# Loading attention pairs over 128 partitions instead of 96, and requesting two FFN weights later

## The chip, the cores and the metric

The kernel runs on one NeuronCore of a Trainium2 chip. The metric is the device time of one execution in microseconds (us). TensorE (PE in the profile) does matrix products and transposes, and loads its stationary operand with separate instructions (PEld). VectorE (DVE), ScalarE (ACT) and GpSimd (POOL) do elementwise work. SyncE (SP) and GpSimd issue most DMA transfers. SBUF is the on-chip memory with 128 partitions, and PSUM holds what TensorE writes.

## The reference

Attention with "beacon" keys and values ahead of the ordinary ones, and then a feed-forward network (FFN) that takes the maximum of three projections:

```python
B, H, S, Nb, D = 8, 8, 576, 16, 64
k_all, v_all = concat(beacon_k, k), concat(beacon_v, v)       # 592 keys
scores = q @ k_all.T / sqrt(D)                                # causal mask on the 576 ordinary keys
a = exp(scores - max); a /= a.sum() + 1e-9
x = heads_joined(a @ v_all)                                   # 4608 tokens x 512
h = maximum(maximum(x @ w1, x @ w2), x @ w3)                  # 4608 x 768
out = h @ w_out                                               # 4608 x 512
```

All inputs and the output are float32. The kernel computes in bfloat16 with float32 sums.

## The kernel before

The unit of attention is a pair: two heads of one batch, 32 pairs in all, four to a batch (`PPB`). Two pairs make a quad. For a pair, q and k must lie with the head dimension along the partitions: two heads of 64 fill 128 partitions, so `qT` is 128 x 576 and `kT` is 128 x 592 (beacons first). There are four of each (`NT`), used in turn.

The pairs get there in three ways. Batch 0 (pairs 0 to 3) is loaded in halves and turned on TensorE by `turn_half`. Pairs 4 to 15 (batches 1 to 3; `B_PE` is 4) are loaded by `load_pair` (L172), cast to bfloat16 by GpSimd in `cast_piece` (L215), turned on TensorE in `turn` (L344), and copied out of PSUM by `evac_q` and `evac_k` (L382, L392). Pairs 16 to 31 use the same load and cast, are stored to DRAM in bfloat16 and fetched by a transposing DMA (L328 to L340).

For a pair of the second kind, partition p of 96 (`QP`) holds six consecutive tokens (`QR`) of both heads. Each token slot r is turned as a 96 x 128 block, so q and k take six transposes each; the copy out of PSUM puts the tokens back in order by a strided view.

The scores of a pair are made in four groups (`emit_scores`, L442): matmuls into one of two PSUM buffers named `sc`, then an exponential on ScalarE. GpSimd zeroes the masked part with affine_select (`emit_masks`, L467, L480). `emit_pv` (L500) multiplies the exponentials with ones, for the sums, and with the values (L524); `invert_sums` and `multiply` divide, and write the FFN's input `xT`. FFN units follow as their tokens become ready: `mm1_halves` (L603) for the first two weights of token block 0, `mm1_unit` (L584) for the rest, and `mm2_unit` (L620) for the output product. For block 0, the first L584 unit is the first that reads the third weight, and the first L620 the first that reads `w_out_sb`.

The order on every engine is written out by hand. `first_steps` (L794) is the list for batch 0. After it, each pair p from 4 has two steps, (p, 0) and (p, 1); in each come the scores of two groups, their masks, a part of `emit_pv` of an earlier quad, then transposes, FFN units and what `plan` holds for that step. In step (p, 0), `turn_pair` turns pair p + 1. Each engine carries out its own instructions in this order and waits at semaphores for the others. GpSimd runs masks, casts and the issues of the weight DMAs on one queue: `load_w` (L282) issues two DMAs for one of the three weights, `load_w_out` (L289) one. All pair loads, value loads and output stores are issued by SyncE, in the order of the list `loads` (L702): pairs 4 and 5, then pair 6, the values of batch 1, and pairs 7 and on. A stage buffer `st` (eight of them) holds one pair or part of the values of a batch.

Of the kernel before, what the change touches and what calls it, by code (L numbers as in the profile page):

```python
# [9 lines left out]
BF16 = mybir.dt.bfloat16  # L10
# [6 lines left out]
def kernel(  # L17
# [13 lines left out]
    nc = tc.nc  # L31

    B, H, S, D = q.shape
    Nb = beacon_k.shape[2]
    NK = S + Nb
    scale = 1.0 / float(D) ** 0.5
    d_model, d_ff = moe_w1.shape
# [6 lines left out]

    QR = 6
    QP = S // QR
    HR = QR // 2
    HALF = S // 2  # L50


    n_kt = (NK + 127) // 128
    NKP = 128 * n_kt
# [5 lines left out]
    PPB = H // 2  # L60
# [4 lines left out]
    B_PE = 4  # L65
# [55 lines left out]
    ffn_psum = ctx.enter_context(tc.tile_pool(name="ffn_psum", bufs=2, space=PSUM))  # L121
# [16 lines left out]
    ident = const.tile([128, 128], BF16, name="ident")  # L138
# [2 lines left out]


    NT = 4
    qTs = [const.tile([128, S], BF16, name=f"qT{i}") for i in range(NT)]
    kTs = []
    for i in range(NT):
        z = const.tile([128, NKP], BF16, name=f"kT{i}")
        nc.vector.memset(z[:, NK:NKP], 0.0)
        nc.vector.memset(z[:, Nb + HALF : 384], 0.0)
        kTs.append(z)  # L150
    nc.vector.memset(ones, 1.0)
    tri = const.tile([128, 128], BF16, name="tri")

    def pv_bank(i, shape, dtype):
        return pv_psum.tile(shape, dtype, name=f"pv{i}")
# [3 lines left out]
    by_pool = nc.gpsimd.tensor_copy  # L159

    STW = 4 * QR * D
    NQ2 = 2 * QR * D
    stage = {}
    v_tiles = {}

    def new_stage(key):
        stage[key] = st_pool.tile([128, STW], FP32, name="st")
        return stage[key]  # L170

    def load_pair(p, gate=None):  # L172
        b, g, j0 = place(p)
        hs = slice(head(g, j0), head(g, j0) + 2)
        st = new_stage(("pair", p))

        if gate:
            gate.memset(st[0:QP, 0:1], 0.0)
        for i, src in enumerate((q, k)):
            nc.sync.dma_start(  # L180
                out=st[0:QP, i * NQ2 : (i + 1) * NQ2].rearrange("p (h x) -> p h x", h=2),
                in_=src[b, hs].rearrange("h (p r) d -> p h (r d)", r=QR),
            )
# [28 lines left out]
            for j in range(PPQ):  # L212
                stage["half16", PPQ * g + j, h, i] = t16[:, 2 * j : 2 * j + 2]

    def cast_piece(p, i, cast):  # L215
        st = stage["pair", p]
        t16 = pair_pool.tile([QP, QR, 2, D], BF16, name=f"p16{i}")
        cast(  # L218
            t16.rearrange("p r h d -> p h r d"),
            st[0:QP, i * NQ2 : (i + 1) * NQ2].rearrange("p (h r d) -> p h r d", h=2, r=QR),  # L220
        )
        stage["pair16", p, i] = t16

    def cast_pair(p, q_cast, k_cast):
        cast_piece(p, 0, q_cast)
        cast_piece(p, 1, k_cast)
        stage.pop(("pair", p))

    V_PIECES = [(0, 3), (3, n_kt)]

# [111 lines left out]


    def turn(p, i, ps):  # L344
        src = stage.pop(("pair16", p, i))
        for r in range(QR):
            nc.tensor.transpose(  # L347
                ps[:, r * QP : (r + 1) * QP],
                src[:, r].rearrange("p h d -> p (h d)"),
                ident[0:QP, 0:QP],  # L350
            )

    def fill(ps, n):
        for i in range(n):
            x0 = 512 + 128 * (i % 4)
            nc.tensor.transpose(ps[:, x0 : x0 + 128], busy[:, 0:128], ident)
# [24 lines left out]

    def evac_q(p, ps, copy):  # L382
        copy(
            qTs[p % NT].rearrange("d (p r) -> d p r", r=QR),
            ps.rearrange("d (r p) -> d p r", r=QR),
        )

    def place_beacons(p, copy):
        b, pi = divmod(p, PPB)
        copy(kTs[p % NT][:, 0:Nb], bT[:, pi, Nb * b : Nb * (b + 1)])  # L390

    def evac_k(p, ps, copy):  # L392
        kT = kTs[p % NT]
        copy(
            kT[:, Nb:NK].rearrange("d (p r) -> d p r", r=QR),
            ps.rearrange("d (r p) -> d p r", r=QR),
        )

    def turn_apart(p, i):
        ps = ffn_psum.tile([128, S], BF16, name="fps")  # L400
        turn(p, i, ps)
        (evac_q, evac_k)[i](p, ps, by_dve)
        if i == 1:
            place_beacons(p, by_act)

    def turn_pair(p, q_copy, shared=True):
        if shared:
            ps = sc_psum.tile([128, 2, 1024], BF16, name="sc")
            banks = [ps[:, i, 0:S] for i in range(2)]
        else:  # L410
            banks = [pv_bank(i, [128, 1024], BF16)[:, 0:S] for i in range(2)]
        for i in range(2):
            turn(p, i, banks[i])
        evac_k(p, banks[1], by_dve)
        evac_q(p, banks[0], q_copy)
# [283 lines left out]
    def load_pairs(p0, p1):  # L699
        return [L(load_pair, p) for p in range(p0, p1)]  # L700
# [79 lines left out]
    def G(p):  # L780
        return L(load_pair, p, nc.vector)
# [7 lines left out]
    def F(n):  # L789
        return lambda: [emit_ffn(END) for _ in range(n)]  # L790
# [16 lines left out]
        ((2, 3), [P(0, 1, False, 0, 2), F(1), M(2, 3)]),  # L807
        ((3, 1), [P(0, 1, False, 2, 4), M(3, 1, True), G(5), F(1), L(turn_beacons, 1, B_PE, bk16_1)]),
        ((3, 2), [F(1), finish_pv, next_7, M(3, 2)]),
        ((3, 3), [F(2), M(3, 3), L(cast_pair, 4, by_pool, by_pool), L(load_w, 2, 0, d_ff), P(1, 1),  # L810
                  L(turn_apart, 4, 0), L(turn_apart, 4, 1), finish_pv, F(1), L(cast_pair, 5, by_pool, by_pool)]),
    ]
    at_step(4, 0, C(cast_pair, 6, by_pool, by_pool))
    at_step(5, 0, C(cast_v, 1, 0, by_pool))
    at_step(5, 0, L(load_w_out))
    at_step(5, 1, C(cast_v, 1, 1, by_pool))
    at_step(5, 1, C(cast_pair, 7, by_pool, by_pool))
    for p in range(8, B_PE * PPB):
        at_step(p - 2, 1, C(cast_pair, p, by_pool, by_pool))
    for b in range(2, B):  # L820
        p = b * PPB
# [6 lines left out]
    for b in range(B_PE, B):  # L828
        p = b * PPB
# [9 lines left out]
    def emit_all():  # L839
# [107 lines left out]
```

## Time and profile before

| What | Value |
|---|---|
| Time, median of 5 runs | 302.04 us (301.32 to 307.57) |
| Profiled execution: time, span | 301.66 us, 299.9 us |
| Mean granted TensorE clock | 0.989 |
| TensorE busy | 284.6 us (95%) |
| GpSimd busy | 127.6 us (43%) |
| L347 transposes of pairs 4 to 15 | 12 a pair |
| L218 casts of a pair's half on GpSimd | 822 ns each, 56 of them |
| L394 copy of k from PSUM (VectorE) | 754 ns |
| L383 copy of q from PSUM (ScalarE) | 640 ns |
| Third weight (two DMAs): issued, median to landing | 31.29 and 31.84 us, 8.8 us |
| Output weight: issued, to landing | 43.90 us, 14.1 us |

Times inside the execution count from the start of the span. "Idle before" is the time for which an engine stood before an instruction, with what released it. The granted clock is the share of TensorE's full clock that the chip allowed. A group's mean is the length of one instruction; matmuls overlap, so their start-to-start distance is shorter than that.

### The profile page before, as it was taken

What the parts mean: (1) busy time and instruction counts of PE and PEld (TensorE: products, weight loads), DVE (VectorE), ACT (ScalarE), POOL (GpSimd) and SP (SyncE); (2) the same over time, 40 slices, a digit from 0 to 9 for tenths busy, and PEclk for the clock granted to TensorE, in tenths of its full rate; (3) what the DMA queues carried; (4) which work ended last, traced back from release to release, by engine and by line L of the source; (5) the groups of instructions that cost most, each with busy time, mean ns of one, the idle gap of its engine ahead of it and who ended that gap; (6) DMA issues with size and microseconds to landing.
All of it is one profiled execution on the core that took longest, in us unless ns stands there. A gap on an engine that the chain in (4) does not pass through costs nothing.

```text
span 299.9 us, 8667 instructions
## 1 busy us (share of the span) xinstructions
PE 284.6 (95%) x3571; PEld 154.6 (52%) x3601; DVE 172.4 (57%) x343; ACT 146.6 (49%) x237; POOL 127.6 (43%) x253
## 2 busy tenths in 40 slices
PE   8879969999999999999999999999999999999995
PEld 4547645554554545454545777545454544444442
DVE  3756633545767475636573757465746575274373
ACT  3685673875665564536463646354635531401300
POOL 7182855566566584556455545552243210000000
PEclk9999995999999999999999999999999999999999
DMA  8999999999999999999999999993212001103003
GB/s 145 186 183 229 213 222 249 256 225 289 217 252 240 210 286 181 192 194 304 235 186 218 298 242 185 153 264 88 42 52 90 2 3 68 74 1 123 19 0 141
DMA packets 85321, 50.68 MB, mean 169 GB/s; under 512 B 64417, under 2 KB 80033, under 8 KB 85281
## 3 DMA queue, kind: packets, MB, share of 16 engines
q1 hardware_dynamic: 80672, 45.76, 69.4%
q0 software_dynamic: 4048, 4.03, 8.2%
q8 instruction: 28, 0.46, 0.7%
q10 hardware_dynamic: 560, 0.33, 0.5%
q14 instruction: 13, 0.10, 0.1%
HBM read 35.13 MB, written 14.22 MB: 165 GB/s over the span
## 4 chain that ended last, share of the span: by engine, by line
PE 82%; DMA 9%; ACT 2%; DVE 2%; POOL 2%; issue 1%; SPq 0%; POOLq 0%; DVEq 0%
PE fps L584 31%; PE sc L584 12%; PE pv L524 12%; PE fps L620 11%; PE sc L452 8%; DMA st<-in_v_dram 4%; PE sc L620 4%; DMA quad<-in_k_dram 3%; DMA st<-in_k_dram 2%; ACT at_sb L461 2%; PE sc L347 2%; DVE xT L556 1%; POOL quad L209 1%; DVE y L628 1%; PE fps L603 1%
## 5 line engine op out<-in xcount | busy, mean ns | idle before, releaser
L461 ACT ACTIVATE at_sb<-sc 128x928 bf16<-128x928 f32 (+5 forms) x128 | 103.9, 863 | 83.7 <-PE sc L452 83.1
L584 PE MATMUL fps<-xT,w_sb 128*128 128x512 bf16 (+1 forms) x464 | 107.1, 358 | 2.2 <-issue 1.0
L480 POOL TENSOR_SCALAR_AFFINE_SELECT at_sb<-at_sb 128x256 bf16<-128x256 bf16 (+2 forms) x148 | 53.8, 382 | 99.5 <-ACT at_sb L461 99.5
L584 PEld LDWEIGHTS <-w_sb 128*128 128x128 bf16 x672 | 61.8, 98 | 65.8 <-issue 12.9
L594 DVE TENSOR_TENSOR hT<-hT,fps 128x512 bf16<-128x512 bf16 x70 | 48.0, 687 | 29.8 <-PE fps L584 29.5
L218 POOL CAST p<-st 96x768 bf16<-96x768 f32 x56 | 44.6, 822 | 0.9 <-DMA st<-in_q_dram 0.5
L584 PE MATMUL sc<-xT,w_sb 128*128 128x512 bf16 (+1 forms) x187 | 42.9, 356 | 0.1
L452 PE MATMUL sc<-qT,kT 64*128 64x288 bf16 (+5 forms) x400 | 35.8, 277 | 2.3 <-ACT at_sb L461 2.2
L620 PE MATMUL fps<-w_out_sb,hT 128*128 128x512 bf16 x143 | 34.6, 379 | 0.9 <-issue 0.6
L620 PEld LDWEIGHTS <-hT 128*128 128x128 bf16 x210 | 19.9, 98 | 24.0 <-DVE hT L594 2.1
L594 DVE TENSOR_TENSOR hT<-hT,sc 128x512 bf16<-128x512 bf16 x32 | 22.0, 688 | 16.9 <-PE sc L584 11.3
L628 DVE COPY y<-fps 128x512 f32<-128x512 f32 x25 | 17.3, 692 | 23.5 <-PE fps L620 22.9
L592 DVE CAST hT<-fps 128x512 bf16<-128x512 f32 x32 | 22.1, 691 | 12.3 <-PE fps L584 12.2
L524 PE MATMUL pv<-at_sb,v_sb 128*32 128x288 bf16 (+5 forms) x1376 | 29.1, 231 | 0.0
L556 DVE TENSOR_TENSOR xT<-pv,recip 128x288 bf16<-128x288 f32 (+2 forms) x93 | 27.2, 347 | 2.7 <-ACT recip L546 2.7
L452 PEld LDWEIGHTS <-kT 64*128 64x128 bf16 x400 | 14.4, 94 | 26.7 <-issue 23.0
L524 PEld LDWEIGHTS <-v_sb 128*32 128x32 bf16 (+1 forms) x1408 | 24.7, 97 | 2.0 <-issue 0.6
L524 PE MATMUL pv<-at_sb,ones 128*32 128x288 bf16 (+4 forms) x500 | 17.6, 256 | 2.5 <-POOL at_sb L480 2.5
L263 POOL CAST v_sb<-st 128x1536 bf16<-128x1536 f32 (+2 forms) x21 | 18.4, 893 | 3.1 <-DMA st<-in_v_dram 3.1
L544 ACT ACTIVATE lnd<-pv 128x288 f32<-128x288 f32 x31 | 13.0, 418 | 10.7 <-PE pv L524 10.7
L524 PEld LDWEIGHTS <-ones 128*32 128x32 bf16 (+2 forms) x512 | 10.9, 95 | 10.0 <-issue 8.3
L592 ACT CAST hT<-sc 128x512 bf16<-128x512 f32 x6 | 3.5, 587 | 23.7 <-PE sc L584 23.7
(74 smaller groups left out, 163.9 us busy)
## 6 DMA issues: line engine op xcount, KB each, us to landing
out_dram<-y SPq DMA_DIRECT2D x35, 256.0 KB, 3.5
st<-in_q_dram SPq DMA_DIRECT2D x28, 288.0 KB, 5.9
st<-in_k_dram SPq DMA_DIRECT2D x28, 288.0 KB, 6.3
st<-in_v_dram SPq DMA_DIRECT2D x24, 256.0 KB, 5.4
w_sb<-in_moe_w_dram POOLq DMA_DIRECT2D x6, 384.0 KB, 7.0
q_dram<-p SPq DMA_DIRECT2D x16, 144.0 KB, 3.2
k_dram<-p SPq DMA_DIRECT2D x16, 144.0 KB, 2.7
st<-in_v_dram SPq DMA_DIRECT2D x8, 224.0 KB, 5.5
```

The costliest lines, as they stand in the source:

```text
L218: cast(t16.rearrange("p r h d -> p h r d"), st[0:QP, i * NQ2 : (i + 1) * NQ2].rearrange("p (h r d) -> p h r d", h=2, r=QR),)
L263: cast(v_sb[0:n, t:t1].rearrange("p t h d -> p (t h d)"), st[0:n, (t - t_lo) * H * D : (t1 - t_lo) * H * D],)
L452: nc.tensor.matmul(ps[:, e, off : off + q1 - q0], kT[hs, 128 * t : 128 * t + 128], qT[hs, q0:q1], start=True, stop=True, tile_position=(64 ...
L461: nc.scalar.activation(out=both_heads(p, gi), in_=ps[:, :, 0 : g_width(p, gi)], func=AF.Exp, scale=scale)
L480: nc.gpsimd.affine_select(out=view, in_=view, compare_op=ALU.is_ge, fill=0.0, base=x0, pattern=[[0, 2], [1, hi - lo]], channel_multiplier=-1,)
L524: nc.tensor.matmul(ps[bank][32 * j : 32 * j + 32, lo + q0 - qa : lo + qb - qa], lhsT, at_view(PPQ * quad + j // 2, t, j % 2, q0, qb), star ...
L556: nc.vector.tensor_mul(xT[:, 2 * g + part - 1, c0 + ca : c0 + cb], ps[bank][:, lo : lo + cb - ca], recip[:, ca:cb],)
L584: nc.tensor.matmul(ps[:, o0 : o0 + n], w_in[i][:, ct, 128 * ft : 128 * (ft + 1)], xT[:, ct, x0 : x0 + n], start=(ct == 0), stop=(ct == n_c ...
L592: (by_act if alone[0] else by_dve)(h, ps)
L594: nc.vector.tensor_max(h, h, ps)
L620: nc.tensor.matmul(ps, hT[:, ft, 128 * tt : 128 * (tt + 1)], w_out_sb[:, ft, :], start=(ft == 0), stop=(ft == n_ft - 1),)
L628: nc.vector.tensor_copy(y, ps)
```

## The change

It has two parts.

The first is the layout of pairs 4 to 15. A load now puts tokens 0 to 511 on all 128 partitions, four consecutive tokens to a partition (`WR` = 4, 1 KB of a head in one run instead of 1.5 KB), for q and for k. The last 64 tokens (`REST`) of q go to partitions 0 to 63, and those of k to partitions 64 to 127 of the same columns. A pair takes four DMAs instead of two. GpSimd casts it with three instructions: q, k, and the common rest. TensorE turns four full 128 x 128 blocks of q, and then four of k and the common one. The copies out of PSUM are one for q's 512 columns, one for k's 512, and one with two pieces of 64 columns for both rests; for that, `qT` and `kT` are now views of one tile `qkT`. Pairs 16 to 31 keep their layout, in a cast tile that now holds q and k together.

The second is the order on GpSimd's queue. The third weight is requested at step (4, 1), after that step's masks, instead of between the casts of pairs 4 and 5. The output weight is requested at step (6, 0) instead of (5, 0).

```diff
+    WR = 4
+    WIDE = 128 * WR
+    REST = S - WIDE
...
-    qTs = [const.tile([128, S], BF16, name=f"qT{i}") for i in range(NT)]
...
+    qkTs = [const.tile([128, S + NKP], BF16, name=f"qkT{i}") for i in range(NT)]
+    qTs = [z[:, 0:S] for z in qkTs]
+    kTs = [z[:, S : S + NKP] for z in qkTs]
...
+    def load_wide(p, gate=None):
...
+        W = 2 * WR * D
+        for i, src in enumerate((q, k)):
+            nc.sync.dma_start(
+                out=st[:, i * W : (i + 1) * W].rearrange("p (h x) -> p h x", h=2),
+                in_=src[b, hs, 0:WIDE].rearrange("h (p r) d -> p h (r d)", r=WR),
+            )
+        for i, src in enumerate((q, k)):
+            nc.sync.dma_start(
+                out=st[REST * i : REST * (i + 1), 2 * W : 2 * W + 2 * D].rearrange("p (h d) -> p h d", h=2),
+                in_=src[b, hs, WIDE:S].rearrange("h p d -> p h d"),
+            )
+
     def load_pair(p, gate=None):
+        if p < B_PE * PPB:
+            load_wide(p, gate)
+            return
...
+    def cast_wide(p, cast):
+        st = stage.pop(("pair", p))
+        t16 = pair_pool.tile([128, 2 * QR, 2, D], BF16, name="p16")
+        W = 2 * WR * D
+        for i in range(2):
+            cast(
+                t16[:, WR * i : WR * (i + 1)].rearrange("p r h d -> p h r d"),
+                st[:, i * W : (i + 1) * W].rearrange("p (h r d) -> p h r d", h=2, r=WR),
+            )
+        cast(t16[:, 2 * WR].rearrange("p h d -> p (h d)"), st[:, 2 * W : 2 * W + 2 * D])
+        stage["wide16", p] = t16
...
     def turn(p, i, ps):
-        src = stage.pop(("pair16", p, i))
-        for r in range(QR):
+
+        src = stage["wide16", p]
+        slots = [(r, WR * i + r) for r in range(WR)] + ([(WR, 2 * WR)] if i == 1 else [])
+        for r, slot in slots:
             nc.tensor.transpose(
-                ps[:, r * QP : (r + 1) * QP],
-                src[:, r].rearrange("p h d -> p (h d)"),
-                ident[0:QP, 0:QP],
-            )
+                ps[:, r * 128 : (r + 1) * 128],
+                src[:, slot].rearrange("p h d -> p (h d)"),
+                ident,
+            )
...
     def evac_k(p, ps, copy):
-        kT = kTs[p % NT]
         copy(
-            kT[:, Nb:NK].rearrange("d (p r) -> d p r", r=QR),
-            ps.rearrange("d (r p) -> d p r", r=QR),
+            kTs[p % NT][:, Nb : Nb + WIDE].rearrange("d (p r) -> d p r", r=WR),
+            ps[:, 0:WIDE].rearrange("d (r p) -> d p r", r=WR),
         )
+        step = S + Nb
+        x0 = S + NKP - 2 * step
+        copy(
+            qkTs[p % NT][:, x0:].rearrange("d (i x) -> d i x", i=2)[:, :, WIDE - x0 : S - x0],
+            ps[:, WIDE : WIDE + 2 * REST].rearrange("d (i x) -> d i x", i=2),
+        )
...
-        ((3, 3), [F(2), M(3, 3), L(cast_pair, 4, by_pool, by_pool), L(load_w, 2, 0, d_ff), P(1, 1),
+        ((3, 3), [F(2), M(3, 3), L(cast_pair, 4, by_pool, by_pool), P(1, 1),
...
-    at_step(5, 0, L(load_w_out))
+    at_step(4, 1, L(load_w, 2, 0, d_ff))
...
+    at_step(6, 0, L(load_w_out))
```

More of the change, by code (lines that the diff above doesn't have):

```diff
@@ L143 @@
     NT = 4
-    qTs = [const.tile([128, S], BF16, name=f"qT{i}") for i in range(NT)]
-    kTs = []
-    for i in range(NT):
-        z = const.tile([128, NKP], BF16, name=f"kT{i}")
+    qkTs = [const.tile([128, S + NKP], BF16, name=f"qkT{i}") for i in range(NT)]
+    qTs = [z[:, 0:S] for z in qkTs]
+    kTs = [z[:, S : S + NKP] for z in qkTs]
+    for z in kTs:
         nc.vector.memset(z[:, NK:NKP], 0.0)
         nc.vector.memset(z[:, Nb + HALF : 384], 0.0)
-        kTs.append(z)
     nc.vector.memset(ones, 1.0)
@@ L170, in new_stage @@
         return stage[key]
+    def load_wide(p, gate=None):
+        b, g, j0 = place(p)
+        hs = slice(head(g, j0), head(g, j0) + 2)
+        st = new_stage(("pair", p))
+        if gate:
+            gate.memset(st[:, 0:1], 0.0)
+        W = 2 * WR * D
[9 more added lines that the diff above has]
+            )
     def load_pair(p, gate=None):
+        if p < B_PE * PPB:
+            load_wide(p, gate)
+            return
         b, g, j0 = place(p)
@@ L213, in load_quad @@
                 stage["half16", PPQ * g + j, h, i] = t16[:, 2 * j : 2 * j + 2]
[L215 to L220, printed above, removed]
-        )
-        stage["pair16", p, i] = t16
-    def cast_pair(p, q_cast, k_cast):
-        cast_piece(p, 0, q_cast)
-        cast_piece(p, 1, k_cast)
-        stage.pop(("pair", p))
+    def cast_wide(p, cast):
[9 more added lines that the diff above has]
+        stage["wide16", p] = t16
+    def cast_pair(p, q_cast, k_cast):
+        if p < B_PE * PPB:
+            cast_wide(p, q_cast)
+            return
+        st = stage.pop(("pair", p))
+        t16 = pair_pool.tile([128, 2 * QR, 2, D], BF16, name="p16")
+        for i, cast in enumerate((q_cast, k_cast)):
+            part = t16[0:QP, QR * i : QR * (i + 1)]
+            cast(
+                part.rearrange("p r h d -> p h r d"),
+                st[0:QP, i * NQ2 : (i + 1) * NQ2].rearrange("p (h r d) -> p h r d", h=2, r=QR),
+            )
+            stage["pair16", p, i] = part
     V_PIECES = [(0, 3), (3, n_kt)]
@@ L344, in turn @@
     def turn(p, i, ps):
-        src = stage.pop(("pair16", p, i))
-        for r in range(QR):
+        src = stage["wide16", p]
+        slots = [(r, WR * i + r) for r in range(WR)] + ([(WR, 2 * WR)] if i == 1 else [])
+        for r, slot in slots:
             nc.tensor.transpose(
-                ps[:, r * QP : (r + 1) * QP],
-                src[:, r].rearrange("p h d -> p (h d)"),
-                ident[0:QP, 0:QP],
-            )
+                ps[:, r * 128 : (r + 1) * 128],
+                src[:, slot].rearrange("p h d -> p (h d)"),
+                ident,
+            )
+        if i == 1:
+            stage.pop(("wide16", p))
     def fill(ps, n):
@@ L383, in evac_q @@
         copy(
-            qTs[p % NT].rearrange("d (p r) -> d p r", r=QR),
-            ps.rearrange("d (r p) -> d p r", r=QR),
+            qTs[p % NT][:, 0:WIDE].rearrange("d (p r) -> d p r", r=WR),
+            ps[:, 0:WIDE].rearrange("d (r p) -> d p r", r=WR),
         )
@@ L392, in evac_k @@
     def evac_k(p, ps, copy):
-        kT = kTs[p % NT]
         copy(
-            kT[:, Nb:NK].rearrange("d (p r) -> d p r", r=QR),
-            ps.rearrange("d (r p) -> d p r", r=QR),
+            kTs[p % NT][:, Nb : Nb + WIDE].rearrange("d (p r) -> d p r", r=WR),
+            ps[:, 0:WIDE].rearrange("d (r p) -> d p r", r=WR),
+        )
[4 more added lines that the diff above has]
+            ps[:, WIDE : WIDE + 2 * REST].rearrange("d (i x) -> d i x", i=2),
         )
     def turn_apart(p, i):
-        ps = ffn_psum.tile([128, S], BF16, name="fps")
+        ps = ffn_psum.tile([128, 1024], BF16, name="fps")
         turn(p, i, ps)
@@ L408, in turn_pair @@
             ps = sc_psum.tile([128, 2, 1024], BF16, name="sc")
-            banks = [ps[:, i, 0:S] for i in range(2)]
+            banks = [ps[:, i] for i in range(2)]
         else:
-            banks = [pv_bank(i, [128, 1024], BF16)[:, 0:S] for i in range(2)]
+            banks = [pv_bank(i, [128, 1024], BF16) for i in range(2)]
         for i in range(2):
```

## The prediction

> **What bounds the kernel now.** First the page's busy times and slices: the matmul engine is the bound.
>
> ```profile
> PE 284.6 (95%) x3571; PEld 154.6 (52%) x3601; DVE 172.4 (57%) x343; ACT 146.6 (49%) x237; POOL 127.6 (43%) x253
> ...
> PE   8879969999999999999999999999999999999995
> ...
> PEclk9999995999999999999999999999999999999999
> DMA  8999999999999999999999999993212001103003
> ```
>
> TensorE is full in nearly every slice; the exception that matters is slice 7 (45 to 52.5 us), where the granted clock is 0.5. The DMA engines are full until about 210 us. Next the list of waits, for what stopped TensorE; only one wait of it is long (total, times, longest).
>
> ```profile
> POOL v_sb L263 <- DMA st<-in_v_dram: 3.1, 1, 3.1
> ...
> PE pv L524 <- POOL at_sb L480: 2.5, 1, 2.5
> ```
>
> Then the timelines of TensorE and GpSimd there (start, length, what).
>
> ```profile
> 42.36 0.38 PE L524 MATMUL pv<-at_sb,ones 128*32 128x288 bf16 x6
> 45.23 0.58 PE L524 MATMUL pv<-at_sb,ones 128*32 128x176 bf16 x6 [2.50 <-POOL at_sb L480]
> ...
> 46.60 1.89 PE L603 MATMUL fps<-xT,w_sb 128*128 128x256 bf16 x8
> 48.28 1.17 PE L347 MATMUL sc<-ident,p 96*128 96x96 bf16 x12
> 49.24 0.63 PE L584 MATMUL fps<-xT,w_sb 128*128 128x512 bf16 x1
> ...
> 42.50 1.46 POOL L263 CAST v_sb<-st 128x1536 bf16<-128x1536 f32 x1 [3.13 <-DMA st<-in_v_dram]
> 43.90 0.85 POOL L290 DMA_DIRECT2D w_out_sb<-in_moe_w_out_dram  x1
> 44.76 0.77 POOL L480 TENSOR_SCALAR_AFFINE_SELECT at_sb<-at_sb 128x256 bf16<-128x256 bf16 x2
> ```
>
> GpSimd waits 3.13 us for batch 1's first values, casts them, issues the output weight, and only then masks pair 5, for which TensorE stands from 42.73 to 45.23. By windows of 1 us the clock is 0.68 in 44-45, 0.50 from 45, 0.91 in 51-52: half from about 44.36 to 51.18. The same eight L603 matmuls take 1.03 us elsewhere and 1.89 here. So the stall costs 2.50 us and half of 45.23 to 51.18, 2.98 us: **5.5 us**. Why the values are late is in the DMA queues from 35 to 40 us, in the first weight group of 30-35 us, and in the page's row of the output weight.
>
> ```profile
> q0 software_dynamic: 278, 0.77, 78.2%
> q1 hardware_dynamic: 1240, 0.31, 34.0%
> ...
> w_sb<-in_moe_w_dram POOLq DMA_DIRECT2D x2, 384.0 KB, 8.8
> ...
> w_out_sb<-in_moe_w_out_dram POOLq DMA_DIRECT2D x1, 768.0 KB, 14.1
> ```
>
> The third weight (q0, issued 31.29) moves 0.77 MB while the values on q1 get 0.31 MB.
>
> [...] 1.63 us were idle when it dropped. [...]
>
> **The change part by part**, against the profiled execution's 301.66 us (span 299.9, 1.8 around it; 0.4 below the median 302.04).
>
> *Transposes.* L347 runs 12 in 0.68 us, the last taking 0.206: 43 ns apart, 516 ns a pair. [...] Twelve pairs: -0.2 us, taken as **0**, on the path.
>
> *Casts on GpSimd.* Before 2 x 0.822 = 1.64 us a pair. After two of 512 columns, like the v_sb cast of 128x512 (0.61), and one of 128: 0.61 - 384 x 0.83 ns (the slope from 512 to 768) = 0.29, in all 1.51. Hidden except where GpSimd is last (below).
>
> *Copies out of PSUM.* L394's 576 columns take 0.754 us, L378's 288 take 0.447: 1.07 ns a column. 512 cost 0.69, 128 another 0.28: +0.21 us of VectorE a pair, 2.5 in all. ScalarE's copy of q waits for VectorE's of k (9.1 us in 9 waits), so it comes about 0.2 later less 0.06 of its own. The cover is the matmuls before the next scores; the tightest place is pair 9, where the copy ends at 77.58 and the scores start at 77.68. Bounds 0 to 0.2 x 11 = 2.2 us; I take **0.3**, because the second score group needs the buffer, not the first.
>
> *Loads.* From 25 to 30 us q1 moved pair loads: 782 packets in 92.6% of 80 engine-us, 95 ns per 1.5 KB. A pair is 384 of them: 2.28 us on 16 engines. After: 512 packets of 1 KB and 256 of 256 bytes (24 ns: 3372 packets in 49.7% of 160 engine-us from 10 to 20). At unchanged bytes per ns 512 x 64 + 256 x 24 ns = 38.9, over 16: 2.43 us. [...] I take 2.2, and -0.4 to +0.2 a pair. Pairs 4 to 6 lie ahead of the values: **-0.3 us** of arrival (-1.1 to +0.5). SP issues 24 more loads at 0.31 to 0.45 us; it is ahead, its blocks being on full queues, so nothing on the path. TensorE's k part now waits for three casts instead of two, in the same 1.5 us.
>
> *Third weight moved* from ahead of pair 5's cast to after pair 4's last masks. The values landed at 30.49 + 11.86 = 42.35 (the chain). Without 0.77 MB at 0.21 MB/us they come 3.7 us earlier, with the loads' 0.3 at 38.4. GpSimd: masks end 37.95, the two issues 39.03 (1.08), pair 5's first masks 40.0, then the cast to 41.5, next masks 41.9 and 42.6 (the exponentials end 42.15). TensorE needs the first at 42.73: the wait is gone, with 0.8 us to spare. **-5.5 us.**
>
> What is late next? At full clock TensorE goes 42.36 + 0.79 (44 pv) + 0.97 = 44.1 to pair 7's transposes. GpSimd gives 42.6 + 1.16 (v casts) + 1.51 = 45.2: 1.2 us, of which 0.5 is filled with the first transposes. **+0.7.** Then L584 at 45.3 needs the third weight. From its first issue to its last landing it took 10.1 us before (31.84 + 9.6 - 31.29); with the median 7.0 it is 7.6. From 37.95 that is 45.5 to 48.1. I take 46.5: **+1.2** (0.2 to 2.8).
>
> *Output weight moved* past pair 5's last masks, v, pair 7 and pair 6's masks: issued 46.2 instead of 43.9. It landed at 58.0, needed at 61.84; now needed at 61.84 - 3.6 = 58.2. With the old 14.1 us it lands 60.3; with 11.5 (halfway to the 8.8 of a third-weight half: it starts later, beside smaller packets, with fewer pairs left in the queue) at 57.7. I take **+0.3** (0 to 2.1).
>
> Later casts and stores see DMA at most 2 us later; pair 8 lands about 5 us before its cast. Nothing.
>
> Sum: -5.5 + 0.7 + 1.2 + 0.3 + 0.3 = -3.0, 301.66 - 3.0 = **298.7 us**. [...] 1.9 us of waits in pieces, between 44.1 and 46.5.
>
> **The rivals.** *The third weight comes late and the clock drops again.* Landing at 48.1 (+2.8) and the old half-clock price +3.0: -5.5 + 0.7 + 2.8 + 3.0 + 0.3 = +1.3, 303.0. For it: the idle 1.9 us are already more than the 1.63 that set it off. Against: they are in pieces, and the values no longer compete.
>
> *The output weight becomes the wait* (slower). It is issued 2.3 us later and needed 3.6 earlier. If it keeps 14.1 us and the issue slips by GpSimd's lateness of 1 us, it lands at 61.3: 3.1 us of idle at its first matmul L620, +3.0 for the clock: 298.7 - 0.3 + 6.1 = 304.5; with a weight wait too, 306. It turns slower than before once that wait with its clock price exceeds 3.3 us, a landing after about 58.5 if the full clock price is due.
>
> *The loads give nothing or the values stay late.* At 2.6 us a pair, and a weight that overlaps the values' end, some 2 us of the wait remain: 300.5.
>
> *All clean.* [...] only the 0.7 and 0.3 remain, 297.2.
>
> **How the numbers follow.** Forecast (297.5 to 300) 0.40; weight late with clock 0.22 (301 to 303.5); output weight 0.16 (303 to 306); loads give nothing 0.10; clean 0.12 (296.3 to 297.5). A measurement of this kernel tells about 1%, 3.0 us, from no change. Under 298.6: half of the forecast, the clean case and the edge of others: 0.38; over 304.7: most of the output-weight case and a little of the late weight: 0.16; between: 0.46. The range 296.6 to 304.3 leaves some 0.05 below and 0.13 above.
>
> **What would show it.** Right: no wait of pv L524 for GpSimd; the v cast's DMA wait under 0.5 us; the transposes nine to a pair in about 0.65 us; waits of L584 for w_sb's DMA and of the transposes for the casts near 45 us; no half clock in slice 7; the first L620 near 58. Wrong: half clock after 44 us, an L620 that waits for w_out_sb's DMA, or waits of scores on pair copies throughout 60 to 120 us.

## Result: 1.2% slower, and where the profile shows it

The changed kernel takes 306.29 us (median of 28 runs), and the kernel before 301.89 us beside it (47 runs). The ratio is 1.0118, 95% interval 1.0095 to 1.0141: slower by 1.2%, 3.6 us, where the prediction had 298.7 us, 3.0 us less than the profiled execution of before, and a range of 296.6 to 304.3. Medians, here and in the table below, are of all runs, while ratios compare only the fast ones, within some 1.5% of their kernel's fastest, so a ratio is not the quotient of two medians. The profiled execution of the changed kernel took 307.17 us (span 305.5), 0.9 us above its median and 5.6 us longer in its span than the one before.

First the page: busy shares of TensorE, granted clock and DMA, each in 40 slices of 7.64 us.

```profile
PE   7879897999948999999999999999999999999995
...
PEclk9999999999996999999999999999999999999999
DMA  7999899996999889999999999995212001202003
```

The half clock of slice 7 is gone. Slices 12 and 13 (84.0 to 99.3 us), full before, now show TensorE at 4 and 8 tenths, and slice 13 the clock at 6. The DMA row, mostly 9 before, has dips to 6 and 8: the engines are no longer always full.

Then the list of waits (total, times, longest).

```profile
ACT qkT L425 <- DVE qkT L441: 13.8, 9, 3.4
...
POOL bk L741 <- DMA bk<-in_beacon_k_dram: 10.2, 2, 9.8
...
PE pv L571 <- POOL at_sb L527: 5.1, 2, 2.9
...
PE sc L387 <- POOL p L250: 1.4, 1, 1.4
```

There is one new wait of GpSimd, 9.8 us long, for the beacons' keys, and TensorE waits twice for GpSimd's masks. The first line is ScalarE's copy of q, which waits for VectorE's copies of k and the rests (9.1 us in the kernel before). (L571, L527 and L741 are the L524, L480 and L694 of before; L631, L667 and L387 are the L584, L620 and L347.)

**The place that the prediction was about.** TensorE's timeline (start, length, what, idle before):

```profile
42.99 0.41 PE L571 MATMUL pv<-at_sb,ones 128*32 128x288 bf16 x12
43.23 0.63 PE L571 MATMUL pv<-at_sb,v_sb 128*32 128x288 bf16 x32
...
47.19 0.23 PE L387 MATMUL sc<-ident,p 128*128 128x128 bf16 x1 [1.37 <-POOL p L250]
47.26 1.03 PE L631 MATMUL fps<-xT,w_sb 128*128 128x512 bf16 x3
...
49.14 0.32 PE L499 MATMUL sc<-qkT 64*128 64x336 bf16 x2 [0.55 <-ACT qkT L425]
```

and GpSimd's:

```profile
38.44 1.08 POOL L323 DMA_DIRECT2D w_sb<-in_moe_w_dram  x2
...
40.48 1.46 POOL L301 CAST v_sb<-st 128x1536 bf16<-128x1536 f32 x1
...
46.84 0.29 POOL L250 CAST p<-st 128x128 bf16<-128x128 f32 x1 [1.47 <-DMA st<-in_k_dram]
...
48.05 0.85 POOL L328 DMA_DIRECT2D w_out_sb<-in_moe_w_out_dram  x1
```

All 12 matmuls with ones run in one stretch: the 2.50 us stall at pair 5 is gone, and with it the 3.13 us for which GpSimd waited for the values. In its place TensorE waits 1.37 us for the cast of pair 7's rest, whose DMA is late, and 0.55 us for a copy out of PSUM. The clock stays full (1.00 in every microsecond from 40 to 54).

**The place that it was not about.** GpSimd, changed kernel:

```profile
78.91 0.29 POOL L250 CAST p<-st 128x128 bf16<-128x128 f32 x1
88.96 0.61 POOL L741 CAST bk<-bk 64x512 bf16<-64x512 f32 x1 [9.76 <-DMA bk<-in_beacon_k_dram]
89.52 1.01 POOL L527 TENSOR_SCALAR_AFFINE_SELECT at_sb<-at_sb 128x224 bf16<-128x224 bf16 x3
90.49 1.58 POOL L261 CAST p<-st 96x768 bf16<-96x768 f32 x2
92.03 0.76 POOL L527 TENSOR_SCALAR_AFFINE_SELECT at_sb<-at_sb 128x256 bf16<-128x256 bf16 x2
```

TensorE, changed kernel:

```profile
89.95 0.30 PE L571 MATMUL pv<-at_sb,ones 128*32 128x288 bf16 x4 [2.91 <-POOL at_sb L527]
92.48 0.58 PE L571 MATMUL pv<-at_sb,ones 128*32 128x176 bf16 x6 [2.23 <-POOL at_sb L527]
```

GpSimd, the kernel before, at the same step:

```profile
80.08 1.59 POOL L218 CAST p<-st 96x768 bf16<-96x768 f32 x2
83.89 0.61 POOL L694 CAST bk<-bk 64x512 bf16<-64x512 f32 x1 [2.22 <-DMA bk<-in_beacon_k_dram]
84.46 1.01 POOL L480 TENSOR_SCALAR_AFFINE_SELECT at_sb<-at_sb 128x224 bf16<-128x224 bf16 x3
```

At step (10, 1) GpSimd casts the beacons' keys of batches 4 to 7, needed much later, and behind that cast in its queue stand pair 11's masks, needed at once. The kernel before already waited 2.22 us there, and masks came just in time. Now GpSimd reaches the cast at 79.20 instead of 81.67 (2.47 us earlier: the gain at pair 5, less the 0.8 us by which this execution started later), and the last beacons land at 88.81 instead of 83.75 (5.06 us later): 2.22 + 2.47 + 5.06 = 9.75, the new wait. TensorE stands for 2.91 + 2.23 = 5.14 us, and the clock is half from 90.9 to 97.7 (0.50 in the window 91 to 92, 0.63 in 97 to 98), 3.4 us more.

**Why the beacons are late** is in SyncE's queue (start, length of the issue): changed kernel, one pair's four loads and the first of the next; then the beacons.

```profile
58.33 4.01 SPq L285 DMA_DIRECT2D st<-in_v_dram  x5
...
67.07 0.54 SPq L185 DMA_DIRECT2D st<-in_q_dram  x1
67.66 0.47 SPq L185 DMA_DIRECT2D st<-in_k_dram  x1
68.18 0.61 SPq L190 DMA_DIRECT2D st<-in_q_dram  x1
68.83 0.61 SPq L190 DMA_DIRECT2D st<-in_k_dram  x1
69.55 0.53 SPq L185 DMA_DIRECT2D st<-in_q_dram  x1
...
84.27 1.92 SPq L334 DMA_DIRECT2D bk<-in_beacon_k_dram  x4
```

The kernel before:

```profile
63.97 0.45 SPq L180 DMA_DIRECT2D st<-in_k_dram  x1
64.52 0.40 SPq L180 DMA_DIRECT2D st<-in_q_dram  x1
64.96 0.45 SPq L180 DMA_DIRECT2D st<-in_k_dram  x1
...
78.52 2.35 SPq L296 DMA_DIRECT2D bk<-in_beacon_k_dram  x4
```

A pair now keeps SyncE busy from 67.07 to 69.55, 2.48 us, where its two loads before took 0.40 + 0.45 and their gaps. The beacons are issued 5.75 us later; from the last issue to the last landing it takes 3.05 us (3.30 before). So the beacons land late because they are issued late, not through their own transfer. The transfers of pairs became faster: from 46 to 49 us the queue moves 0.99 MB, 330 KB/us, against 1.12 MB from 25 to 30 us before, 224 (with 107.2% and 92.6% of the 16 engines' time in its packets, so a part of the difference is that the engines were fuller).

The stream falls behind in two steps. Ahead of the line at 58.33, SyncE stood for 4.02 us until a load that it had issued at 49.06 landed, at 58.31. The kernel before waited for landings at that place too, and the changed one is only 1.17 us behind it when it comes to pair 12's first load, here in the changed kernel and in the one before:

```profile
62.44 2.73 SPq L185 DMA_DIRECT2D st<-in_q_dram  x1
```

```profile
61.27 0.64 SPq L180 DMA_DIRECT2D st<-in_q_dram  x1
```

The other 4.58 us come between there and the beacons' issue. In that stretch the queue of these loads, q1, was full before and is no longer full (changed kernel from 62 to 84 us, then before from 61 to 78: packets, MB, share of the 16 engines' time):

```profile
q1 hardware_dynamic: 9398, 4.68, 82.6%
```

```profile
q1 hardware_dynamic: 6875, 4.28, 105.7%
```

So the transfer no longer set the rate there. The issues of pairs 12 to 15, 4 x 2.48 us, are nearly half of the 21.83 us. Some single issues took long as well (2.73 us at 62.44, 3.41 us for two outputs at 79.57), and the profile does not settle what those stood for.

A ruler for the experiments: the span is cut at pair 4's transposes (L387 or L347 into `fps`) and at the first output product (L667 or L620). Before: 30.94, then 30.90 to the output product, then 238.06 to the end. After: 31.74, 27.64, 246.12 (spans are known to 0.1 us). The middle gained 3.26 us, the end lost 8.06; with the 0.80 of the start, which no part of this reading explains, that is the 5.6 us between the spans. The start differs between executions of one kernel; in the profiled executions of the experiments it lies between 31.06 and 37.78. A late start may give the loads time to run ahead (an argument that no run shows by itself), so middles are best compared where the starts are alike.

### The profile page after: what moved, and what is told of

Its sections match the earlier page's. It is cut to its first block, busy times and chain, and to the rows that moved or that the text cites. A ratio compares the mean times of both kernels' runs of the same rounds, so it can differ in the third digit from the quotient of the medians.

```text
span 305.5 us, 8623 instructions
## 1 busy us (share of the span) xinstructions
PE 284.8 (93%) x3535; PEld 154.4 (51%) x3565; DVE 174.4 (57%) x355; ACT 145.6 (48%) x237; POOL 125.5 (41%) x265
## 4 chain that ended last, share of the span: by engine, by line
PE 78%; DMA 6%; SPq 5%; DVE 3%; ACT 3%; issue 2%; POOL 2%; POOLq 0%; ACTq 0%; DVEq 0%
PE fps L631 29%; PE sc L631 12%; PE pv L571 11%; PE fps L667 10%; PE sc L499 7%; PE sc L667 4%; DMA quad<-in_k_dram 3%; DMA st<-in_k_dram 2%; SPq L285 2%; ACT at_sb L508 2%; PE sc L387 2%; SPq L185 1%; DMA bk<-in_beacon_k_dram 1%; SPq L190 1%; DVE xT L603 1%
## 5 line engine op out<-in xcount | busy, mean ns | idle before, releaser
L631 PE MATMUL fps<-xT,w_sb 128*128 128x512 bf16 (+1 forms) x464 | 107.7, 359 | 2.2 <-issue 1.0
L527 POOL TENSOR_SCALAR_AFFINE_SELECT at_sb<-at_sb 128x256 bf16<-128x256 bf16 (+2 forms) x148 | 54.0, 384 | 101.3 <-ACT at_sb L508 101.1
L631 PEld LDWEIGHTS <-w_sb 128*128 128x128 bf16 x672 | 62.1, 98 | 65.7 <-issue 13.2
L631 PE MATMUL sc<-xT,w_sb 128*128 128x512 bf16 (+1 forms) x187 | 42.9, 356 | 0.1
L499 PE MATMUL sc<-qkT 64*128 64x288 bf16 (+5 forms) x400 | 35.9, 277 | 2.9 <-ACT at_sb L508 2.2
L667 PE MATMUL fps<-w_out_sb,hT 128*128 128x512 bf16 x143 | 34.6, 379 | 0.8 <-issue 0.6
L667 PEld LDWEIGHTS <-hT 128*128 128x128 bf16 x210 | 19.9, 98 | 24.0 <-DVE hT L641 2.1
L571 PE MATMUL pv<-at_sb,v_sb 128*32 128x288 bf16 (+5 forms) x1376 | 29.1, 231 | 0.0
L499 PEld LDWEIGHTS <-qkT 64*128 64x128 bf16 x400 | 14.7, 94 | 27.3 <-issue 23.6
L571 PEld LDWEIGHTS <-v_sb 128*32 128x32 bf16 (+1 forms) x1408 | 24.7, 97 | 2.0 <-issue 0.6
L261 POOL CAST p<-st 96x768 bf16<-96x768 f32 x32 | 25.4, 821 | 0.0
L571 PE MATMUL pv<-at_sb,ones 128*32 128x288 bf16 (+4 forms) x500 | 17.8, 257 | 5.2 <-POOL at_sb L527 5.1
L571 PEld LDWEIGHTS <-ones 128*32 128x32 bf16 (+2 forms) x512 | 11.1, 95 | 12.8 <-issue 11.1
```

The source lines that it names most:

```text
L261: cast(part.rearrange("p r h d -> p h r d"), st[0:QP, i * NQ2 : (i + 1) * NQ2].rearrange("p (h r d) -> p h r d", h=2, r=QR),)
L499: nc.tensor.matmul(ps[:, e, off : off + q1 - q0], kT[hs, 128 * t : 128 * t + 128], qT[hs, q0:q1], start=True, stop=True, tile_position=(64 ...
L527: nc.gpsimd.affine_select(out=view, in_=view, compare_op=ALU.is_ge, fill=0.0, base=x0, pattern=[[0, 2], [1, hi - lo]], channel_multiplier=-1,)
L571: nc.tensor.matmul(ps[bank][32 * j : 32 * j + 32, lo + q0 - qa : lo + qb - qa], lhsT, at_view(PPQ * quad + j // 2, t, j % 2, q0, qb), star ...
L631: nc.tensor.matmul(ps[:, o0 : o0 + n], w_in[i][:, ct, 128 * ft : 128 * (ft + 1)], xT[:, ct, x0 : x0 + n], start=(ct == 0), stop=(ct == n_c ...
L667: nc.tensor.matmul(ps, hT[:, ft, 128 * tt : 128 * (tt + 1)], w_out_sb[:, ft, :], start=(ft == 0), stop=(ft == n_ft - 1),)
```

## Experiments

Theory after the comparison: a pair's four DMAs make SyncE's stream of loads late, and GpSimd, which works in order, waits for it ahead of masks. Rivals: the wide layout costs time throughout, or the moved weight requests delay the loads. "Middle" and "end" are the two parts of the span named above, from one profiled execution; ratios are to the kernel before, run beside each (medians 301.62 to 302.17), with the 95% interval.

| Kernel | Median, us (runs) | Ratio | Middle | End |
|---|---|---|---|---|
| before | 301.89 (47) | 1 | 30.90 | 238.06 |
| changed | 306.29 (28) | 1.0118 [1.0095, 1.0141] | 27.64 | 246.12 |
| e1 changed, beacons' cast later | 304.27 (4) | 1.011 [1.0028, 1.0192] | 26.41 | 240.64 |
| e2 moved requests alone | 304.01 (20) | 1.0024 [0.9995, 1.0053] | 31.95 | 238.11 |
| e3 wide loads alone | 307.63 (4) | 1.0172 [1.0100, 1.0245] | 29.56 | 243.39 |
| e4 before, four DMAs a pair | 303.25 (20) | 1.0034 [1.0002, 1.0065] | 30.08 | 240.30 |
| e5 changed, both casts later | 299.84 (15) | 0.9943 [0.9913, 0.9972] | 29.86 | 237.84 |
| e6 before, both casts later | 300.79 (12) | 0.9989 [0.9956, 1.0022] | 28.69 | 237.95 |
| e7 changed, no rest loads | 301.58 (20) | 0.9974 [0.9948, 1.0000] | 29.75 | 238.53 |
| e8 changed, output weight put back | 306.04 (4) | 1.0128 [1.0064, 1.0191] | 28.55 | 244.07 |
| e9 e2 with both casts later | 301.77 (10) | 0.9987 [0.9946, 1.0027] | 31.12 | 237.89 |
| e10 e3 with both casts later | 301.65 (20) | 1.0004 [0.9977, 1.0030] | 27.69 | 237.87 |
| e11 e5 once more | 300.77 (22) | 0.9941 [0.9912, 0.9969] | 26.14 | 237.88 |

### The number of DMAs by itself: e4

The kernel before, with its 1.5-KB rows on 96 partitions, but one DMA for each head.

```diff
+        if p < B_PE * PPB:
+            for i, src in enumerate((q, k)):
+                for e in range(2):
+                    x0 = i * NQ2 + e * QR * D
+                    nc.sync.dma_start(
+                        out=st[0:QP, x0 : x0 + QR * D],
+                        in_=src[b, head(g, j0) + e].rearrange("(p r) d -> p (r d)", r=QR),
+                    )
+            return
```

> The kernel before, but each load of pairs 4 to 15 is issued as two DMAs, one a head: four DMAs a pair, same packets of 1.5 KB, same 96 partitions, same transposes. Theory, the number of SyncE's DMAs (issue time, and few DMAs in flight) makes the stream late: beacons land 2 to 4 us later than before (86 to 88 us instead of 83.8), GpSimd's wait for them grows from 2.2 to 4 to 6 us; time 301 to 304 us. Rival, it is the 256-byte rows and the 128-partition layout: beacons within 1 us of before, time 300.5 to 301.5 us.

Measured: 303.25 us, ratio 1.0034. GpSimd's timeline, and TensorE's:

```profile
79.94 1.59 POOL L227 CAST p<-st 96x768 bf16<-96x768 f32 x2
87.77 0.61 POOL L703 CAST bk<-bk 64x512 bf16<-64x512 f32 x1 [6.24 <-DMA bk<-in_beacon_k_dram]
```

```profile
91.29 0.56 PE L533 MATMUL pv<-at_sb,ones 128*32 128x176 bf16 x6 [2.03 <-POOL at_sb L489]
```

The same bytes in the same rows, in twice as many DMAs, bring the beacons late enough that GpSimd casts them at 87.77 instead of 83.89, and make a wait of 6.24 us and a stall of 2.03 us at the same place. The number of DMAs is sufficient to make the stream late and to stall TensorE, without the wide layout and without the moved requests. It does not bring the whole loss: the end is 2.24 us longer here, and 8.06 in the changed kernel. Nor does it separate the time that SyncE needs for an issue from the smaller number of bytes that are under way at once. The stall is shorter than in the changed kernel, in line with TensorE coming later to it: pair 5's stall is still there (2.23 us).

### Without the DMAs of the rest: e7

```diff
-        for i, src in enumerate((q, k)):
-            nc.sync.dma_start(
-                out=st[REST * i : REST * (i + 1), 2 * W : 2 * W + 2 * D]...
-                in_=src[b, hs, WIDE:S].rearrange("h p d -> p h d"),
-            )
...
-        cast(t16[:, 2 * WR].rearrange("p h d -> p (h d)"), st[:, 2 * W : 2 * W + 2 * D])
+        cast(t16[:, 2 * WR].rearrange("p h d -> p (h d)"), st[:, 2 * W - 2 * D : 2 * W])
```

> The changed kernel without the loads of the last 64 tokens of q and k of pairs 4 to 15 (24 DMAs of 32 KB; the rest's cast reads columns of q that are there, so those tokens are wrong). SyncE issues two DMAs a pair again, casts, transposes and copies are as changed. Theory, SyncE's DMA count: the last beacons land at 78 to 83 us instead of 88.8, pair 7's third cast waits for no load, no wait near 90 us; from the first output product to the end 238 to 239 us; time 296.5 to 298.5. Rival, the weights' transfers or the large loads themselves make the stream late: beacons after 86 us, time above 301.

Measured: 301.58 us, ratio 0.9974: below the changed kernel, but not the 296.5 to 298.5 that was expected. The beacons land at 78.81, ten us earlier than in the changed kernel and five earlier than before, and GpSimd doesn't wait (11% of the pairs' bytes are gone too, some 0.8 MB, which at 330 KB/us is 2.4 us of the ten):

```profile
80.50 0.29 POOL L245 CAST p<-st 128x128 bf16<-128x128 f32 x1
80.74 0.61 POOL L736 CAST bk<-bk 64x512 bf16<-64x512 f32 x1
```

The end takes 238.53, as in the kernel before. The middle takes 29.75, 2.1 us more than in the changed kernel, and takes a part of the expected gain: TensorE waits 2.51 us there, followed by 3.41 us of half clock:

```profile
48.56 0.61 PE L626 MATMUL fps<-xT,w_sb 128*128 128x512 bf16 x2 [2.51 <-DMA w_sb<-in_moe_w_dram]
```

Here the third weight is late, the wait that the prediction feared. That the wide loads run ahead of it when SyncE doesn't hold them up is the author's estimate; it was not tried.

All thirteen profiled executions fall in line with the number of DMAs: the beacons' last recorded landing is at 83.5 to 86.1 us with two DMAs a pair (before, e2, e6, e9), at 87.4 to 94.9 with four (changed, e1, e3, e4, e5, e8, e10, e11), and at 78.8 here. Counted from pair 4's transposes it is 51.7 to 52.8, 52.9 to 57.2 and 47.6 us, so one execution with four (e1) is hardly later than those with two.

### The order on GpSimd: e1, e5, e6 and e11

e1 moves the beacons' cast one step on. e5 (and e11, the same kernel) also moves the casts of pairs 16 and on from the first to the second step of a pair. e6 makes both moves in the kernel before.

```diff
-    at_step(B_PE * PPB - 6, 1, L(by_pool, bk16, bk32))
+    at_step(B_PE * PPB - 5, 1, L(by_pool, bk16, bk32))
...
-            at_step(p + i - 5, 0, C(cast_pair, p + i, by_pool, by_pool))
+            at_step(p + i - 5, 1, C(cast_pair, p + i, by_pool, by_pool))
```

> The changed kernel with the cast of the last beacons (bk16) moved from step (10, 1) to (11, 1), behind pair 13's cast, nothing else. Theory, late beacons: the loss is one wait. GpSimd stands 9.8 us for the beacons' DMA ahead of pair 11's masks, TensorE stands 2.9 + 2.2 us for these and runs at half clock afterwards (some 3 us). With the cast behind those masks the waits go, and the time falls by 6 to 8 us to 297 to 299 us. Rival, spread cost (two copies of k, four loads, three casts a pair): the time stays within 1 us of the changed kernel, 304 to 306. Rival, the moved weights: as well 304 to 306.

e1: 304.27 us, where 297 to 299 was expected. The time alone would fit the two rivals; the trace shows something else. The first stall goes, the second stays; GpSimd, then TensorE:

```profile
88.86 1.78 POOL L261 CAST p<-st 96x768 bf16<-96x768 f32 x2 [5.98 <-DMA st<-in_q_dram]
```

```profile
91.05 0.56 PE L571 MATMUL pv<-at_sb,ones 128*32 128x176 bf16 x6 [2.25 <-POOL at_sb L527]
```

The next load in SyncE's order is pair 16's q, and it is just as late; its cast stands ahead of pair 11's second masks. The expectation missed this: it is the stream that is late, not the beacons. So the next edit moved that cast as well.

> The changed kernel with the beacons' cast at (11, 1) and the casts of pairs 16 and on moved from step (p, 0) to (p, 1), so that no mask of pair 11 stands behind a load that is late. Theory, a late load stream ahead of masks on GpSimd's queue: no wait of TensorE for a mask near 90 us, no half clock there; from the first output product to the end of the span 238 to 239 us as in the kernel before (246.1 in the changed one, 240.6 with the beacons' cast alone moved); time 297 to 299 us, 1% faster than before. Rival, the wide layout costs time all along: that stretch stays above 240.5 us and the time at 300 to 304.

> The changed kernel with both casts later, once more, for its profile beside the two others and for a narrower interval. Theory: 298 to 300.5, ratio 0.992 to 0.998; no idle of TensorE over 0.5 us between 75 and 110 and no half clock there. Rival (the first measurement was chance): a ratio of 1.000 or more.

e5: 299.84 us (297 to 299 was expected), 0.6% faster than before and 1.7% faster than the changed kernel; e11: 300.77 against 302.17 for the kernel before beside it, the same ratio (the median lies just above what was expected, the ratio within). GpSimd in e11:

```profile
90.93 1.17 POOL L246 CAST p<-st 128x512 bf16<-128x512 f32 x2
92.04 0.30 POOL L250 CAST p<-st 128x128 bf16<-128x128 f32 x1
92.28 0.61 POOL L741 CAST bk<-bk 64x512 bf16<-64x512 f32 x1
92.84 1.60 POOL L261 CAST p<-st 96x768 bf16<-96x768 f32 x2
```

The casts run without a wait, and the end takes 237.88. Loads, transposes and copies are those of the changed kernel, so the loss of 8 us at the end is the waiting of GpSimd ahead of masks, with the stalls and the half clock that follow from it. Both profiled executions took longer than their medians (306.95 and 303.52 us); they lost it in the first 38 us, where nothing was changed by these edits, and e5 also waited 2.85 us for pair 7's rest with half clock after it, which e11 did not.

> Control: the kernel before with the same two moves of casts. In it no mask was late, so the time is that of before, within 0.5% (300.5 to 302 us), and the stall for batch 1's values near 43 us stays. If the moves themselves gain, it would be 298 to 299.

e6: 300.79 us, the same as before: with its stream on time, the kernel before gains nothing measurable from later casts; its stall for the values stays, 1.69 us.

### The two parts alone: e2, e3, e9 and e10

e2 makes the second part of the change in the kernel before; e3 undoes it in the changed kernel. e9 and e10 are these two with both casts later.

```diff
-        ((3, 3), [F(2), M(3, 3), L(cast_pair, 4, by_pool, by_pool), L(load_w, 2, 0, d_ff), P(1, 1),
+        ((3, 3), [F(2), M(3, 3), L(cast_pair, 4, by_pool, by_pool), P(1, 1),
...
-    at_step(5, 0, L(load_w_out))
+    at_step(4, 1, L(load_w, 2, 0, d_ff))
...
+    at_step(6, 0, L(load_w_out))
```

> The kernel before with only the two weight requests moved, pair loads over 96 partitions as before. Theory, late beacons through SyncE's doubled loads: without those the beacons land near 84 to 85 us, the wait for batch 1's values shrinks to under 1 us, and most of the gain of the prediction stays: 297.5 to 299.5 us. Rival, the moved weights cause the loss: 304 to 306 us. If 96-partition loads keep the values late, 300 to 301.

e2: 304.01 us, ratio 1.0024; not the gain that was expected. The median falls in the rival's range, but the ratio's interval reaches 0.9995, and the trace shows no late beacons. The values' stall goes, and the third weight's comes, with half clock from 52.0 to 58.8:

```profile
50.34 0.39 PE L584 MATMUL fps<-xT,w_sb 128*128 128x512 bf16 x1 [1.20 <-DMA w_sb<-in_moe_w_dram]
52.79 1.03 PE L584 MATMUL fps<-xT,w_sb 128*128 128x512 bf16 x2 [2.05 <-DMA w_sb<-in_moe_w_dram]
```

There is no stall near 90 (end 238.11), so the moved requests alone don't delay the stream by enough.

> The changed kernel with both weight requests put back, so only the layout of the pairs differs from before. Theory, late beacons: TensorE is not early, but SyncE's stream is late; GpSimd waits 4 to 7 us for the beacons, TensorE 0 to 3 us for pair 11's masks, and the first stall for the values stays about 2 us: 301 to 305 us. Rival, the moves of the weights cause the loss: 300.5 to 301.5 us, beacons on time.

e3: 307.63 us, 2.6 above the upper end of what was expected. GpSimd waits 7.94 us for the beacons, and TensorE stalls at the same two places:

```profile
96.07 0.30 PE L571 MATMUL pv<-at_sb,ones 128*32 128x288 bf16 x4 [1.09 <-POOL at_sb L527]
98.60 0.58 PE L571 MATMUL pv<-at_sb,ones 128*32 128x176 bf16 x6 [2.23 <-POOL at_sb L527]
```

The loss sits with the wide loads.

> The kernel before with the moved weight requests alone, and with the beacons' cast at (11, 1) and the casts of pairs 16 and on at the second step of their pair. Theory (the late loads of SyncE's stream cost the changed kernel its gain, and with later casts the moves and the wide loads together are worth about 0.6%; neither alone is): without the wide loads the moved third weight still arrives late for TensorE, a wait of 2 to 3.5 us near 50 with half clock; 300.5 to 304. Rival (the gain of the variant with later casts comes from the moved requests alone): the values' wait goes and nothing takes its place; 297.5 to 299.8.

> The wide loads alone, with the weight requests at their old places, and with the beacons' cast at (11, 1) and the casts of pairs 16 and on at the second step of their pair. Theory: the values' wait near 45 stays (about 2 us, with or without half clock), no idle of TensorE near 90 to 100; 299.5 to 302.5, and at least 4 us faster than the wide loads with the casts at their old places (307.6). Rival (the wide layout itself costs time throughout, by copies and the order of the scores): 304 or more even with later casts.

e9: 301.77 us, ratio 0.9987; TensorE waits 1.15 and 1.67 us for the third weight, with half clock from 47.6 to 54.4. e10: 301.65 us, ratio 1.0004, 6 us below e3; no stall near 90, and one for the values:

```profile
47.02 0.55 PE L571 MATMUL pv<-at_sb,ones 128*32 128x176 bf16 x6 [1.05 <-POOL at_sb L527]
```

So with later casts neither part alone gains anything measurable, and both together gain 0.6% (e5, e11), though e9's interval overlaps theirs. The traces show why: the requests alone exchange the values' stall for the weight's, and in the changed kernel and e11 the weight comes in time (in e1 0.8 us late). Why it does there, but not in e7, was not tried by itself; that SyncE's slow issues leave it room is an argument, no more.

### The output weight's place: e8

```diff
+    at_step(5, 0, L(load_w_out))
...
-    at_step(6, 0, L(load_w_out))
```

> The changed kernel with the output weight requested at step (5, 0) as before, only the third weight moved. In the changed kernel a pair load issued at 49.1 us lands at 58.3, as the output weight's transfer ends. Theory, that transfer is a part of the stream's lateness: the beacons land 1 to 3 us earlier (86 to 88), GpSimd still waits over 5 us for them, TensorE stalls 2 to 4 us in all near 90 us; time 300 to 304 us. If SyncE's count alone does it, the beacons stay at 88.5 and the time at 304 to 306; if the output weight does it all, beacons at 84 and 298 us.

e8: 306.04 us, ratio 1.0128, as the changed kernel; TensorE stalls 0.48 and 2.23 us at the masks near 95, with half clock from 96.4 to 103.2. So the place of the output weight is not the cause of the loss. Whether a part of the lateness comes from it stays open: GpSimd's wait for the beacons is 7.33 us instead of 9.76, and the end 2 us shorter, in an execution that started 6 us later.

## Why the prediction was wrong

**The failed step** is the last one ahead of the sum: "Later casts and stores see DMA at most 2 us later; pair 8 lands about 5 us before its cast. Nothing." It rested on a sentence of the loads' step: "SP issues 24 more loads at 0.31 to 0.45 us; it is ahead, its blocks being on full queues, so nothing on the path." Both were wrong. The issues are longer (0.54, 0.47, 0.61, 0.61; 2.48 us a pair with the gaps), the queue behind them was no longer full (82.6% from 62 to 84 us, where before it was 105.7%), so SyncE and not the transfer set the rate there, and the beacons landed 5.06 us later. Pair 8's last load landed at 49.46, only 1.6 us before its cast at 51.08. How much of the lateness is the length of the issues, and how much what else SyncE stood for, no run separated. The profile before held the warning, the 2.22 us for which GpSimd already waited at L694 ahead of masks: a cast without slack, 40 us behind the place of the change. Every microsecond of gain in the middle and of delay in the stream was added to it. The price was 8.06 us at the end. e4 shows the cause by itself, for 2.24 us of it; in e7, without the extra DMAs, and in e5, e10 and e11, with the casts moved and the loads kept, the price is gone. No rival had it. The nearest had a transfer that becomes late, but the output weight's; its 304.5 to 306 us fit the result by chance, since that weight came before it was needed.

Part by part, the rest:

- **Values' stall and half clock, -5.5.** Right: both are gone. The values' cast starts at 40.48 without a wait, where 40.0 was worked out.
- **What is late next, +0.7 and +1.2.** Right in sum, other in kind: pair 7's casts cost 0.16 us by GpSimd's lateness and 1.37 us by a late DMA, which the sum did not have, and the third weight (landed at 44.47 and 46.54; 46.5 was taken) cost nothing more behind it. The first L631 comes at 47.26, where 46.5 was worked out.
- **Output weight, +0.3.** Landed at 58.51, needed at 59.38: 0.
- **Transposes, 0.** Nine in 0.67 us, against twelve in 0.68: right. They start 56 ns apart (median), as the 26 transposes of L356, of 128 columns too, did in the trace of before.
- **Casts.** 2 x 0.611 + 0.292 = 1.51 us a pair, as worked out.
- **Copies, +0.3.** VectorE takes 0.688 + 0.224 = 0.91 us for k's columns and both rests, +0.16 (+0.21 taken). TensorE waits 0.8 us in two places for the copy of q, 0.5 more than taken.
- **Loads, 2.2 us a pair.** The transfer came out better: 590 KB at 330 KB/us are 1.8 us. That it would take less than the 2.43 at unchanged bytes per ns was the author's estimate, which no trace of before shows, and no run separates what made it faster. But here a pair took the longer of transfer and issue, and the issue was 2.48.
- **Clock.** The sum had no half clock at pair 7 for 1.9 us of waits in pieces, the author's estimate, which no trace of before shows; 1.37 and 0.55 us brought none (the last section has the idle times of both places). The forecast had not looked at the place where the clock did fall, 90.9 us.

The middle came to -3.26 us, where the sum had -3.0. That is in part luck, as 1.53 us for pair 7's casts and 0.8 us for copies stood in for 1.9, 0.3 and 0.3 of partly other kinds. With the casts moved (e5, e11) the time gains 0.6%, some 1.8 us of the 3.0; why not all of it isn't shown. The prediction was right about the place it looked at, and it stopped looking there.

## What to carry to other kernels

When a load is cut into more DMAs, compare the time that the issuing queue needs for a tile with the time of its transfer (here 2.48 us and 1.8 us a pair), and follow what stands behind it in that queue: the beacons, some 40 us behind the place of the change, landed 5.06 us later. Ahead of a change that makes one stretch faster and a stream later, list every wait on that stream in the profile of before, short ones above all, and ask what stands behind each in its engine's order: here a wait of 2.22 us that cost nothing had no slack left. Work that is needed late (here the casts of beacons and of pairs 16 and on) belongs behind work that is needed now.

## What was not expected of the hardware

- The issue of a 64-partition load of two 256-byte pieces took SyncE mostly 601 to 607 ns, longer than one of 128 partitions with 1-KB pieces (median 468 and 541 ns), for an eighth of the bytes.
- The half clock came in stretches of 3.41 us (e4, e7) and 6.83 us (before from 44.36 to 51.19, changed kernel from 90.91 to 97.74), and an idle of the same length did or did not bring it: 2.23 us did in e4, near 45, and 2.25 us did not in e1, near 91. With the small gaps, TensorE was idle for 1.85 us in the 3.41 us ahead of the drop before (the prediction counted the 1.63 of the long wait alone), 3.11 in the changed kernel and 1.79 in e9. At pair 7 in the changed kernel, where the clock stayed full, two stretches of 3.41 us counted back from its drop at 90.91 (43.13 to 46.54 and to 49.95) have 0.91 and 1.25; the most in any 3.41 us there is 1.97, from 45.82, more than the 1.85 that came ahead of half clock before. So neither the longest wait nor the idle sum of just any 3.41 us tells the cases apart. Full clock came back after 3.41 us of half clock with 0.22 us of idle (both kernels), and not after those with 0.89 (before) and 1.59 (changed). No run varied the place of one idle by itself, and what decides it is not shown.
- Executions of one kernel differ in their first 38 us: pair 4's transposes came between 30.94 and 37.78 us in the profiled executions. They came at 34.3 to 34.7 us where half clock had lasted 10.24 us (from 18.3 to 28.5 in e1, and in e2 and e10; mean granted clock of the whole execution 0.983, 0.972 and 0.983), at 37.8 where it had lasted 20.5 and 23.9 (e3, e8; 0.955 and 0.951), and at about 31 where there was none (before, e6; 0.989, with the half clock from 44.36 alone, and 1.000). What decides it was not tried.
